# Attention backward on one core: S in three column tiles of 32 query rows, dP in two of 64 and 32

## The chip, the cores and the metric

The kernel runs on one core of a Trainium2 chip. The metric is the device time in microseconds. Two runs of the kernel before took 1706.85 and 1711.59 us, median 1709.22.

## The reference

Two attention blocks, A and B, of the same shape are computed forward, their outputs are concatenated, and all gradients are returned for a given output gradient. For each block:

```python
B, Sq, D = 8, 96, 640
H, Sk, Dh = 32, 512, 128
q = (x @ wq).reshape(B, Sq, H, Dh).transpose(0, 2, 1, 3)
scores = einsum("bhqd,bhkd->bhqk", q, k_cache) * Dh ** -0.5
p = softmax(scores)
o = einsum("bhqk,bhkd->bhqd", p, v_cache)
out = o.transpose(0, 2, 1, 3).reshape(B, Sq, H * Dh) @ wo
...
# vjp: gradients of x, k_cache, v_cache, wq and wo of both blocks
```

All tensors are bfloat16. There are 2 x 32 x 8 = 512 pairs of head and batch element, each with 96 query rows and 512 keys.

## The kernel before

The kernel walks over ticks, one for each pair (head h, batch element b), block A first and then block B. The function `build_block` registers the pieces of work with an `Emitter` under a tick and a slot; the emitter sorts them and issues them in that order. The pieces of one pair are spread over several ticks by the offsets in `OFF`, so that in one tick PE works on S of one pair, on P of an earlier one and on dS of a still earlier one. Work of a head as a whole (projections, transposes, weight gradients) lies in between.

For one pair the stages are as follows.

- K and V are loaded for two batch elements at a time (`c_ld`, L266, on SP's queue). Their transposes come from a DMA transpose (`c_xt`, L275) into KT and VT, or, for about half of the pairs, K is transposed by PE (`c_s1`, L285) and copied by DVE to `KT_pe` (L287).
- S (`c_s2a`, L298) is one product: the stationary side is the 128 x 96 slice of `QT_h`, the moving side is KT with 512 columns. The result `S_ps` is 96 x 512 in float32, one PSUM bank. DVE takes the negated row maximum `negm` (L300).
- ACT computes the exponential with row sums, `E_sb` (L310); DVE inverts the sums, `rinv` (L320); POOL multiplies, `P_sb` (L329).
- PE transposes P (L365), ACT copies it to `PT_sb` (L378); O comes from V and PT (L359) and goes to `OD` by ACT (L375). dV comes from P and dO (L389), and ACT copies it (L392).
- POOL forms `prod` = O times dO (L407). dP (`c_s6`, L417) is one product: the stationary side is the 128 x 96 slice of `dOT_h`, the moving side VT with 512 columns. Directly behind it on PE comes `dl_ps` (L419), with one moving column, which sums `prod`. DVE makes `dS_sb` = (dP - dl) * P (L421).
- PE transposes dS (L346), DVE copies it (L348), dQ comes from K and the transposed dS (L340). dK comes from dS and Q (L432), and ACT copies it (L435).
- The results dV and dK go out by DMAs issued on POOL's queue (L398).

Around these stand the products of a head: Q and dO projections (`q_ps`, L243), transposes (`n_ps` L258, `nat_ps` L455, `woT_ps` L210, `wqT_ps` L216), weight gradients (`dwo_ps` L470, `dwq_ps` L490), and the output and dx sums over a group of heads (`o_ps`, L512).

All PSUM tiles come from one pool of eight banks (`bank`). S and what follows from it down to P are given a higher priority (`tc.high_priority`), which the framework uses when it orders each engine's instructions. Each `nc.tensor.matmul` becomes a weight load of the stationary side and a product. PE runs them in program order; a load may run while the product before it is still running.

Of the kernel before, what the change touches and what calls it, by code (L numbers as in the profile page):

```python
# [53 lines left out]
def build_block(tc, em, tick0, blk, x, kc, vc, wq, wo, g_all, out_all, dx, dk, dv, dwq, dwo, ident, ones, pools, HG=6, first=True, groups=None):  # L54
    nc = tc.nc
    B, Sq, D = x.shape
# [19 lines left out]
    while t0 < T:  # L76
        w = 512 if T - t0 >= 512 else (256 if T - t0 >= 256 else (128 if T - t0 >= 128 else T - t0))
# [4 lines left out]
    while c0 < D:  # L82
        w = 512 if D - c0 >= 512 else (256 if D - c0 >= 256 else 128)
# [14 lines left out]
    def bank(shape, dt, name):  # L98
        return ps.tile(shape, dt, name=name, tag="bank")
# [191 lines left out]
    def c_s2a(h, b):  # L291
        def f():
            with tc.high_priority(PRIO_OFF):
                st = CS[(blk, h, b)]
                hs = HS[(blk, h)]
                tok = slice(b * Sq, (b + 1) * Sq)
                S_ps = bank([Sq, Sk], F32, "S_ps")
                nc.tensor.matmul(S_ps[:], hs["QT_h"][:, tok], st["KT"], start=True, stop=True)  # L298
                negm = wk.tile([Sq, 1], F32, name="negm", bufs=3)
                nc.vector.tensor_reduce(negm[:], S_ps[:], axis=AX.X, op=ALU.max, negate=True)  # L300
                st["S_ps"], st["negm"] = S_ps, negm
        return f
# [108 lines left out]
    def c_s6(h, b):  # L411
        def f():
            st = CS[(blk, h, b)]
            hs = HS[(blk, h)]
            tok = slice(b * Sq, (b + 1) * Sq)
            dP_ps = bank([Sq, Sk], F32, "dP_ps")
            nc.tensor.matmul(dP_ps[:], hs["dOT_h"][:, tok], st["VT"], start=True, stop=True)  # L417
            dl_ps = bank([Sq, 1], F32, "dl_ps")
            nc.tensor.matmul(dl_ps[:], st["prod"][:], ones[:, 0:1], start=True, stop=True)  # L419
            dS_sb = wk.tile([Sq, Sk], BF16, name="dS_sb", bufs=3)  # L420
            nc.vector.scalar_tensor_tensor(dS_sb[:], dP_ps[:], dl_ps[:, 0:1], st["P_sb"][:], op0=ALU.subtract, op1=ALU.mult)  # L421
            st["dS_sb"] = dS_sb
        return f
# [318 lines left out]
```

## Time and profile before

| what | value |
|---|---|
| runs | 1706.85 and 1711.59 us, median 1709.22 |
| profiled execution | span 1699.8 us from the first to the last instruction |
| PE products | 22024, busy 1675.7 us (99%) |
| PE weight loads | 22024, busy 1343.8 us (79%) |
| ACT, DVE, POOL busy | 1405.2, 1329.8, 1040.3 us |
| S products (L298) | 512, two groups of 268 and 244 by the source of KT, mean 380 and 379 ns |
| dP products (L417) | 512, mean 382 ns |
| weight loads for S and dP | 512 each, mean 122 and 123 ns |
| DMA | 423.05 MB, mean 249 GB/s |
| granted TensorE clock | 0.998 of full |

The profile shows one execution. It has no time of that execution other than its span, which lies 9.4 us below the median of the runs; that much lies around the instructions. A duration of a product is from its start to its modelled end, and products overlap; the distance from one start to the next tells how long PE is taken by it. PE and PEld are two rows of one engine: the products and the loads of their stationary sides.

### The profile page before, as it was taken

Reading aid. Unit: us, or ns where it says so; the run is one execution under the profiler, and the core shown is the slowest. Engines: PE = TensorE matmul, PEld = TensorE weight load, DVE = VectorE, ACT = ScalarE, POOL = GpSimd, SP = SyncE. Lnnn points to the kernel's source line nnn. Section 1 sums busy time; section 2 is a strip of 40 time slices with the busy share of each in tenths; the row PEclk is TensorE's granted clock in tenths of the full one; section 3 lists DMA queues with packets and bytes.
Section 4 is the critical chain, followed back from the end, with each engine's and each line's share of the span. In section 5 each row is a group of like instructions: output and inputs, shape, how many; then the busy total and the mean of one; then the engine's idle time right before and its main releaser. Section 6 shows DMA issues by size and latency. Waiting matters only on the chain.

```text
span 1699.8 us, 56567 instructions
## 1 busy us (share of the span) xinstructions
PE 1675.7 (99%) x22024; PEld 1343.8 (79%) x22024; DVE 1329.8 (78%) x3052; ACT 1405.2 (83%) x3518; POOL 1040.3 (61%) x1747
## 2 busy tenths in 40 slices
PE   8999999999999999999999999999999999999999
PEld 7877778778778778777778877887788778778876
DVE  6887678878788878787778876787788778878877
ACT  6998889869869869878768998897799679878975
POOL 3676567646647647656566764675576557656754
PEclk9999999999999999999999999999999999999999
DMA  9999999999999999999999999999899989999994
GB/s 256 252 259 250 258 225 260 262 242 243 262 221 252 268 238 259 225 251 237 281 256 269 273 270 248 238 289 248 218 261 276 237 221 261 281 217 240 263 247 141
DMA packets 600429, 423.05 MB, mean 249 GB/s; under 512 B 419360, under 2 KB 557984, under 8 KB 600160
## 3 DMA queue, kind: packets, MB, share of 16 engines
q1 hardware_dynamic: 546576, 242.08, 72.2%
q0 software_dynamic: 53584, 177.35, 32.7%
q8 instruction: 173, 2.83, 0.7%
q14 instruction: 96, 0.79, 0.2%
HBM read 161.09 MB, written 159.12 MB: 188 GB/s over the span
## 4 chain that ended last, share of the span: by engine, by line
PE 89%; DMA 4%; ACT 3%; issue 1%; DVE 1%; POOL 0%; SPq 0%; DVEq 0%; ACTq 0%; POOLq 0%
PE q_ps L243 12%; PE o_ps L512 12%; PE dwo_ps L470 6%; PE dV_ps L389 6%; PE dK_ps L432 6%; PE S_ps L298 6%; PE dP_ps L417 6%; PE dwq_ps L490 6%; PE x_ps L340 5%; PE x_ps L365 5%; PE dst_ps L346 5%; PE x_ps L359 5%; PE kT_ps L285 3%; PE n_ps L258 3%; PE nat_ps L455 2%; DMA VT<-V_sb 1%
## 5 line engine op out<-in xcount | busy, mean ns | idle before, releaser
L329 POOL TENSOR_SCALAR P_sb<-E_sb,rinv 96x512 bf16<-96x512 bf16 x512 | 352.6, 689 | 567.8 <-DVE rinv L320 559.2
L310 ACT ACTIVATE E_sb<-S_ps,negm 96x512 bf16<-96x512 f32 x512 | 351.0, 686 | 187.6 <-DVE negm L300 181.9
L421 DVE SCALAR_TENSOR_TENSOR dS_sb<-dP_ps,dl_ps,P_sb 96x512 bf16<-96x512 f32 x512 | 382.1, 746 | 60.9 <-PE dl_ps L419 54.6
L300 DVE TENSOR_REDUCE negm<-S_ps 96x1 f32<-96x512 f32 x512 | 347.6, 679 | 50.9 <-PE S_ps L298 46.6
L435 ACT ACTIVATE dK_sb<-dK_ps 128x512 bf16<-128x512 f32 x512 | 302.1, 590 | 63.4 <-PE dK_ps L432 56.5
L392 ACT ACTIVATE dV_sb<-dV_ps 128x512 bf16<-128x512 f32 x512 | 311.6, 609 | 0.0
L378 ACT ACTIVATE PT_sb<-x_ps 128x384 bf16<-128x384 bf16 x512 | 253.1, 494 | 0.0
L512 PEld LDWEIGHTS <-OD 128*128 128x128 bf16 x1536 | 132.2, 98 | 100.4 <-issue 1.0
L398 POOL DMA_DIRECT2D out_dram<-dV_sb x256 | 194.9, 761 | 11.8 <-issue 8.6
L398 POOL DMA_DIRECT2D out_dram<-dK_sb x256 | 195.0, 762 | 9.1 <-issue 4.4
L389 PE MATMUL dV_ps<-dOnat_h,P_sb 96*128 96x128 bf16 x2048 | 198.2, 219 | 0.8 <-DVE dOnat_h L160 0.6
L417 PE MATMUL dP_ps<-VT,dOT_h 128*96 128x512 bf16 x512 | 195.4, 382 | 3.0 <-DMA VT<-V_sb 3.0
L432 PE MATMUL dK_ps<-Qnat_h,dS_sb 96*128 96x128 bf16 x2048 | 198.1, 219 | 0.1
L407 POOL TENSOR_TENSOR prod<-OD,dOT_h 128x96 bf16<-128x96 bf16 x512 | 184.2, 360 | 13.8 <-ACT OD L375 12.6
L348 DVE COPY dST_sb<-dst_ps 128x384 bf16<-128x384 bf16 x512 | 177.1, 346 | 10.5 <-PE dst_ps L346 10.3
L365 PE MATMUL x_ps<-ident,P_sb 96*128 96x96 bf16 x2048 | 172.0, 205 | 0.8 <-POOL P_sb L329 0.3
L359 PE MATMUL x_ps<-PT_sb,V_sb 128*128 128x96 bf16 x2048 | 172.3, 206 | 0.2 <-ACT PT_sb L378 0.2
L346 PE MATMUL dst_ps<-ident,dS_sb 96*128 96x96 bf16 x2048 | 172.3, 206 | 0.2 <-DVE dS_sb L421 0.2
L340 PE MATMUL x_ps<-dST_sb,K_sb 128*128 128x96 bf16 x2048 | 171.0, 206 | 1.3 <-ACT dK_sb L435 0.8
L375 ACT ACTIVATE OD<-x_ps 128x192 bf16<-128x192 f32 (+1 forms) x515 | 167.9, 326 | 3.9 <-PE x_ps L340 3.9
L320 DVE RECIPROCAL rinv<-rowsum 96x1 f32<-96x1 f32 x512 | 79.9, 156 | 106.0 <-ACT E_sb L310 100.4
L340 PEld LDWEIGHTS <-K_sb 128*128 128x128 bf16 x2048 | 131.1, 98 | 25.1 <-issue 1.6
(84 smaller groups left out, 3744.4 us busy)
## 6 DMA issues: line engine op xcount, KB each, us to landing
out_dram<-dV_sb POOLq DMA_DIRECT2D x256, 256.0 KB, 5.2
out_dram<-dK_sb POOLq DMA_DIRECT2D x256, 256.0 KB, 5.3
K_sb<-in_A_k_cache_dram SPq DMA_DIRECT2D x128, 256.0 KB, 5.3
V_sb<-in_A_v_cache_dram SPq DMA_DIRECT2D x128, 256.0 KB, 5.2
K_sb<-in_B_k_cache_dram SPq DMA_DIRECT2D x128, 256.0 KB, 5.0
V_sb<-in_B_v_cache_dram SPq DMA_DIRECT2D x128, 256.0 KB, 4.9
out_dram<-dwo_sb POOLq DMA_DIRECT2D x63, 160.0 KB, 4.8
out_dram<-dwq_sb POOLq DMA_DIRECT2D x31, 320.0 KB, 6.1
```

The lines of the kernel that those rows point to most:

```text
L300: nc.vector.tensor_reduce(negm[:], S_ps[:], axis=AX.X, op=ALU.max, negate=True)
L310: nc.scalar.activation(E_sb[:], st["S_ps"][:], ACT.Exp, bias=st["negm"][:], scale=1.0, accum_out=rowsum[:])
L329: pinned(nc.gpsimd.tensor_scalar(P_sb[:], st["E_sb"][:], st["rinv"][:], 0.0, op0=ALU.mult, op1=ALU.add))
L340: nc.tensor.matmul(dQT_ps, st["K_sb"][:, c, :], st["dST_sb"][:, c * Sq:(c + 1) * Sq], start=(c == 0), stop=(c == KC - 1))
L389: nc.tensor.matmul(dV_ps[:, c * 128:(c + 1) * 128], P_sb[:, c * 128:(c + 1) * 128], hs["dOnat_h"][:, b * 128:(b + 1) * 128], start=True, s ...
L392: nc.scalar.activation(SB[(blk, h, b // 2, "v")][:, b % 2], dV_ps[:], ACT.Identity, scale=1.0)
L398: pinned(nc.gpsimd.dma_start(dst[b - 1:b + 1, h].rearrange("b (p c) d -> p b (c d)", c=KC), SB.pop((blk, h, b // 2, which))[:]))
L417: nc.tensor.matmul(dP_ps[:], hs["dOT_h"][:, tok], st["VT"], start=True, stop=True)
L421: nc.vector.scalar_tensor_tensor(dS_sb[:], dP_ps[:], dl_ps[:, 0:1], st["P_sb"][:], op0=ALU.subtract, op1=ALU.mult)
L432: nc.tensor.matmul(dK_ps[:, c * 128:(c + 1) * 128], dS_sb[:, c * 128:(c + 1) * 128], hs["Qnat_h"][:, b * 128:(b + 1) * 128], start=True, s ...
L435: nc.scalar.activation(SB[(blk, h, b // 2, "k")][:, b % 2], dK_ps[:], ACT.Identity, scale=1.0)
L512: nc.tensor.matmul(o_ps[:], src[:, t * 128:(t + 1) * 128], rhs, start=(hh == 0), stop=(hh == groups[g] - 1))
```

## The change

S is computed by three products, each for 32 of the 96 query rows, and dP by two, for 64 and 32 rows. Every product takes its own slice of the stationary side and writes its own rows of the same PSUM tile. The moving side is the same in all of them. A product whose output has 32 or 64 rows uses as many columns of the array, at the position given by the first output row: S uses 128 x 32 parts at columns 0, 32 and 64, dP a 128 x 64 part at column 0 and a 128 x 32 part at column 64. Nothing else is edited.

```diff
@@ c_s2a
                 S_ps = bank([Sq, Sk], F32, "S_ps")
-                nc.tensor.matmul(S_ps[:], hs["QT_h"][:, tok], st["KT"], start=True, stop=True)
+                for j in range(0, Sq, 32):
+                    nc.tensor.matmul(S_ps[j:j + 32, :], hs["QT_h"][:, b * Sq + j:b * Sq + j + 32], st["KT"], start=True, stop=True)
                 negm = wk.tile([Sq, 1], F32, name="negm", bufs=3)
@@ c_s6
             dP_ps = bank([Sq, Sk], F32, "dP_ps")
-            nc.tensor.matmul(dP_ps[:], hs["dOT_h"][:, tok], st["VT"], start=True, stop=True)
+            for j, w in ((0, 64), (64, Sq - 64)):
+                nc.tensor.matmul(dP_ps[j:j + w, :], hs["dOT_h"][:, b * Sq + j:b * Sq + j + w], st["VT"], start=True, stop=True)
             dl_ps = bank([Sq, 1], F32, "dl_ps")
```

## The prediction

> **What bounds the kernel now.** I read the head of the page first: which engine is full, and at which clock.
>
> ```profile
> span 1699.8 us, 56567 instructions
> PE 1675.7 (99%) x22024; PEld 1343.8 (79%) x22024; DVE 1329.8 (78%) x3052; ACT 1405.2 (83%) x3518; POOL 1040.3 (61%) x1747
> PEclk9999999999999999999999999999999999999999
> PE 89%; DMA 4%; ACT 3%; issue 1%; DVE 1%; POOL 0%; SPq 0%; DVEq 0%; ACTq 0%; POOLq 0%
> ```
>
> PE is busy for 99% of the span at full clock in every slice, and it holds 89% of the chain that ended last. A busy PE can still be waiting inside its pipeline, so the next view is the list of who waited for whom on PE; its longest entries are these.
>
> ```profile
> PE dP_ps L417 <- DMA VT<-V_sb: 3.0, 2, 2.4
> PE tp_ps L134 <- DMA ld_tmp<-in_grad_out_dram: 2.7, 1, 2.7
> PE S_ps L298 <- DMA KT<-K_sb: 2.1, 1, 2.1
> ```
>
> All waits of PE together are under 20 us. So time is set by how fast products follow each other, which is read from start times in the timeline, not from durations. This is PE in an ordinary tick:
>
> ```profile
> 805.51 0.34 PE L365 MATMUL x_ps<-ident,P_sb 96*128 96x96 bf16 x4
> 805.68 0.39 PE L389 MATMUL dV_ps<-dOnat_h,P_sb 96*128 96x128 bf16 x4
> 805.90 0.38 PE L417 MATMUL dP_ps<-VT,dOT_h 128*96 128x512 bf16 x1
> 806.12 0.16 PE L419 MATMUL dl_ps<-ones,prod 128*96 128x1 bf16 x1
> 806.15 0.49 PE L455 MATMUL nat_ps<-ident,OD 128*128 128x128 bf16 x6
> ```
>
> Four products of 128 columns take 0.22 us from start to start, 55 ns each; dP with 512 columns takes 0.22 us; dl with one column 0.03 us, though it lasts 0.16. The distance follows the number of moving columns: (220 - 55) / (512 - 128) = 0.43 ns a column, with a floor of about 26 ns. It does not ask how many columns the stationary side has: S and dP have 96 of them, the others 128. The rest of a duration (380 - 216 = 164 ns for dP, the same as the whole of dl) overlaps the next product. I use 216 ns for the stream of one 512-column product.
>
> How weights are loaded is seen where a product leaves no time for it:
>
> ```profile
> 39.84 0.38 PE L417 MATMUL dP_ps<-VT,dOT_h 128*96 128x512 bf16 x1
> 39.84 0.13 PEld L419 LDWEIGHTS <-prod 128*96 128x96 bf16 x1
> 40.06 0.17 PE L419 MATMUL dl_ps<-ones,prod 128*96 128x1 bf16 x1
> 40.06 0.12 PEld L298 LDWEIGHTS <-QT_h 128*96 128x96 bf16 x1
> 40.09 0.40 PE L298 MATMUL S_ps<-KT_pe,QT_h 128*96 128x512 bf16 x1
> ```
>
> The load for the next product begins when the present one starts, and 30 ns (26 unrounded) after its load S starts. So loads of 0.12 us are pipelined too, and hidden except for the floor.
>
> **What the change adds.** In the program as built, PE's order is that of before with each S replaced by three load-and-product pairs and each dP by two: 3 x 512 = 1536 products and 1536 loads more. S uses a part of the array 32 columns wide at columns 0, 32 and 64; dP uses one 64 wide at 0, then one 32 wide at 64. All else uses the full 128. Every piece still moves all 512 columns of K or V, so the work saved is nil: a tile of 32 query rows streams as long as one of 96. The queues of SP and POOL are unchanged; on DVE some hundred neighbouring instructions change places. I cost those at nothing, because DVE is idle for 22% of the span; with that cover gone each would cost at most one DVE instruction, 0.7 us, some 70 us in all.
>
> **Term 1, further starts of S.** Low bound: a tile starts as soon as its weights are in, 26 ns after the last one (the dl row), and streams beside it: 2 x 26 = 52 ns. High bound: it waits for the stream before, as every product in the trace does: 2 x 216 = 432 ns. I take the low end: the three write different rows of one bank and hold different columns of one mode, so nothing that the rows show in use is shared but the moving operand. That choice is worth (432 - 52) x 512 = 195 us. The Trainium skill, "TensorE: Matmul & The Clock Gate", section "Measured speedup vs the span model", says that tiles in different columns run together, three of them 2.38 times as fast as in sequence, about 4 ns apart. By it this term would be 8 ns; no row here can show it.
>
> **Term 2, the second start of dP.** The bounds are 26 and 216 ns. Here the two pieces have different widths, so they lie in two modes of the array, and I take 216: they follow each other.
>
> **Term 3, changing the width.** S goes from 128 to 32 and back, two changes; dP goes to 64, to 32, to 128, three. The trace shows no such change: all its products use the whole array. Low bound 0: the new product starts on the heels of the old. High bound 190 ns: everything of the old product ends first (164 ns after its stream), and then the new weights are loaded (26). Between these I take 80 ns, by the rows of the durations. A one-column product lasts 164 ns and a load of 96 columns 123, of which 96 x 0.43 = 41 are columns and 82 the way in; 164 - 82 is about 80 ns, what a product has to do in the array and behind it once its last column is there. If the way in may overlap and the array must be empty, that is the gap. The Trainium skill speaks against this change here: "TensorEngine Tiling (Array Packing)", section "Key Properties", says that changing the tiling mode drains the engine, tile changes within a mode do not. It has no duration; by it the zero end of this term would be out.
>
> **The sum.** S: 52 + 2 x 80 = 212 ns. dP: 216 + 3 x 80 = 456 ns. Together 668 ns, 512 times: 342 us. All of it lies on the path, since PE has no idle time to take it. Span 1699.8 + 342 = 2042 us. The median of the runs, 1709.2, lies 9.4 us above the profiled span; with that, 2051 us, which I give as 2050.
>
> **Who waits for later results.** In the tick shown, S starts at 804.33, negm ends at 805.50, E at 806.27, P at 807.36, and PE first uses P at 808.71: 1.3 us of room against 0.2 us of delay, and the following tick is itself later by 0.67. dS ends at 807.21 and is first used at 808.14. Neither becomes a wait; without that room the delay would count once more, 0.2 + 0.46 us a tick at most. ACT's 1405 us are 69% of the new span, so no other engine takes over. The distances between PE starts sum to some 61 us more than the columns account for; with slower PE part of this may vanish, which I leave out.
>
> **Rivals.** *Not slower: tiles side by side, widths changed free.* The mechanism is the early loading seen in the rows: if loads for other columns and modes run under the product before, further starts cost between 0 and 26 ns, three of them 0 to 78 ns a pair of S and dP, 1709 to 1749 us, 1729 in the middle. It decides while the pair costs under 67 ns (34 us / 512), 22 ns a start. For it: no row shows weights being waited for, and 96 and 128 stationary columns alternate without a gap. Against it: five changes of width must cost nothing, and the full-width products use the columns that the tiles use. *In sequence, widths free.* S +432, dP +216, 648 ns x 512 = 332 us: 2041 us. For it: every product in the trace starts after the stream before it. Against it: they all use the same columns. It gives nearly my time, with starts 0.22 us apart inside S. *Full drain.* 190 ns a change: S 52 + 380, dP 216 + 570, 1218 ns x 512 = 624 us: 2333 us. For it: the 164 ns after each stream are real latency; against it: at other boundaries the engine overlaps all of it. *Only dP in sequence, no drain.* 268 ns x 512 = 137 us: 1846 us. Sequence and an 80 ns drain together give 1048 ns, 537 us, 2246 us. That the change doesn't split the products can be left out: the program as built has the pieces.
>
> **How the numbers follow.** Forecast, side by side in S with a partial drain (1900 to 2150): 0.38. In sequence without drain: 0.15. Full drain: 0.17. Sequence and drain: 0.08, most of it below 2335. Only dP in sequence: 0.08. Free: 0.14, of which 0.10 stays below 1743 and 0.04 between there and 1749. The range from 1745 to 2335 leaves out some 0.1 at the bottom and 0.08 at the top, where the full drain comes out heavier than 190 ns. A difference of 2% (34 us) is about what a measurement of this kernel tells from no change. Faster by more has no mechanism: no column streamed is saved and PE is full; 0.02. Within 2%: 0.10. Slower: 0.88.
>
> **What would show it.** In the profile after, PE should have 23560 products and stay near full. In the timeline the three S starts should lie about 0.03 us apart, and the next full-width product should start some 0.3 us after the last of them; dP's second piece should start about 0.30 us after the first. S starts 0.22 us apart mean the sequence; starts 0.4 us apart around each change of width mean the full drain. Pieces of dP close together, or a full-width product 0.22 us after the last tile, make the forecast wrong, and so does a clock below full in the PEclk row, since then gaps would have changed the grant.

## The result and the profile after

The changed kernel takes 2062.97 us (median of two runs, 2061.99 and 2063.95) against 1709.22, a ratio of 1.2083 with a 95% interval of 1.2014 to 1.2151. The forecast was 2050. In the changed file S is line 299, dP 419, dl 421.

The head of the page after, to be read against that of before:

```profile
span 2060.2 us, 59424 instructions
PE 2033.2 (99%) x23390; PEld 1365.1 (66%) x23560; DVE 1358.6 (66%) x3052; ACT 1432.0 (70%) x3518; POOL 1042.2 (51%) x1747
PEclk9999999999999999999999999999999999999999
PE 98%; issue 1%; DVE 0%; DMA 0%; POOL 0%; ACT 0%; SPq 0%; DVEq 0%; POOLq 0%
```

The span is 360 us longer, and PE is still full, at full clock. The other engines have the same number of instructions and nearly the same busy time, now a smaller share. There are 23560 weight loads, 1536 more, as the program has them; 170 product records are missing from the trace. So PE itself takes longer for its work, and the place is seen in the timeline. First PE's products, then its loads, in one stretch of the kernel after:

```profile
1001.29 0.39 PE L390 MATMUL dV_ps<-dOnat_h,P_sb 96*128 96x128 bf16 x4
1001.61 0.72 PE L419 MATMUL dP_ps<-VT,dOT_h 128*64 128x512 bf16 x2
1002.26 0.20 PE L421 MATMUL dl_ps<-ones,prod 128*96 128x1 bf16 x1
1002.33 0.44 PE L134 MATMUL tp_ps<-ident,ld_tmp 128*128 128x128 bf16 x5
1002.61 0.38 PE L243 MATMUL q_ps<-gT,woT_h 128*128 128x512 bf16 x1
1002.92 0.40 PE L299 MATMUL S_ps<-KT,QT_h 128*32 128x512 bf16 x3
```

```profile
1001.61 0.11 PEld L419 LDWEIGHTS <-dOT_h 128*64 128x64 bf16 x1
1001.94 0.09 PEld L419 LDWEIGHTS <-dOT_h 128*32 128x32 bf16 x1 [0.23 <-issue]
1002.26 0.12 PEld L421 LDWEIGHTS <-prod 128*96 128x96 bf16 x1 [0.23 <-issue]
1002.91 0.10 PEld L299 LDWEIGHTS <-QT_h 128*32 128x32 bf16 x3 [0.26 <-issue]
1003.24 0.33 PEld L243 LDWEIGHTS <-woT_h 128*128 128x128 bf16 x3 [0.23 <-issue]
```

From dV to dl PE takes 0.97 us (1001.29 to 1002.26); before it took 0.44 (805.68 to 806.12). The second piece of dP starts 0.33 us after the first, and dl 0.32 after the second. The three pieces of S together last 0.40 us, hardly longer than one product, and the next full-width load begins 0.32 us after their first start. In the rows of the loads the reason stands at the end: at a change of width a load no longer begins with the product before it but, where that has 512 columns, 0.30 to 0.33 us behind its start; the row is idle for 0.23 us or more, and the profile finds nothing that it waited for ("issue").

The start times of the trace give the same distances. These are medians over the 512 pairs, in ns from one product's start to the next. In the kernel after, at least 97% of the steps of each row lie within 4 ns of the median; behind S this leaves out 91 steps of some 548 ns, where the next product is one of the missing records.

| step | before | after | more |
|---|---|---|---|
| a 128-column product, then dP | 56 | 149 | 93 |
| dP's first piece to its second | none | 333 | 333 |
| dP's last product to dl | 220 | 320 | 100 |
| dl to the next product | 26 | 66 | 40 |
| into S, from 128 columns / from 512 | 56 / 215 | 149 / 306 | 93 / 91 |
| between S's pieces, twice | none | 3 | 7 |
| S's last product to the next | 216 | 322 | 106 |
| the full-width product behind S to the one after it | 56 to 215, by its columns | 10 or 11 more; 37 more with 96 stationary columns | 14 on average |

S costs 220 ns more, dP and dl 566, together 786 ns; times 512 that is 402 us. The span grew by 360. The other 42 us come back from small waits that PE had before: dl to its follower, for example, had a mean of 46 ns with a median of 26, which is 10 us of 512 steps; after, nearly all are 66. The section on the prices put together follows these waits up.

### The profile page after: what moved, and what is told of

It is laid out like the page before. It is cut to its first block, busy times and chain, and to the rows that moved or that the text cites. A ratio compares the mean times of both kernels' runs of the same rounds, so it can differ in the third digit from the quotient of the medians.

```text
span 2060.2 us, 59424 instructions
## 1 busy us (share of the span) xinstructions
PE 2033.2 (99%) x23390; PEld 1365.1 (66%) x23560; DVE 1358.6 (66%) x3052; ACT 1432.0 (70%) x3518; POOL 1042.2 (51%) x1747
## 4 chain that ended last, share of the span: by engine, by line
PE 98%; issue 1%; DVE 0%; DMA 0%; POOL 0%; ACT 0%; SPq 0%; DVEq 0%; POOLq 0%
PE dP_ps L419 16%; PE q_ps L243 10%; PE o_ps L514 10%; PE S_ps L299 8%; PE dV_ps L390 6%; PE dwo_ps L472 6%; PE dK_ps L434 5%; PE dwq_ps L492 5%; PE x_ps L366 4%; PE x_ps L360 4%; PE dst_ps L347 4%; PE x_ps L341 4%; PE dl_ps L421 3%; PE n_ps L258 3%; PE kT_ps L285 3%; PE nat_ps L457 2%
## 5 line engine op out<-in xcount | busy, mean ns | idle before, releaser
L419 PE MATMUL dP_ps<-VT,dOT_h 128*64 128x512 bf16 (+1 forms) x1024 | 370.1, 396 | 0.0
L419 PEld LDWEIGHTS <-dOT_h 128*64 128x64 bf16 (+1 forms) x1024 | 101.6, 99 | 169.5 <-issue 116.4
L514 PEld LDWEIGHTS <-OD 128*128 128x128 bf16 x1536 | 117.7, 98 | 112.4 <-issue 40.0
```

The lines of the kernel that those rows point to most:

```text
L419: nc.tensor.matmul(dP_ps[j:j + w, :], hs["dOT_h"][:, b * Sq + j:b * Sq + j + w], st["VT"], start=True, stop=True)
L514: nc.tensor.matmul(o_ps[:], src[:, t * 128:(t + 1) * 128], rhs, start=(hh == 0), stop=(hh == groups[g] - 1))
```

## Experiments

Two theories can give a time near 2063. The width theory: each change of the array's width costs about 0.1 us, pieces of one width run side by side, pieces of different widths follow each other. The count theory: each further product has a price, 354 us / 1536 = 230 ns. Each run below was compared with the kernel before on the same chip.

### S alone in pieces

```diff
 # c_s2a as changed, c_s6 as before
-            for j, w in ((0, 64), (64, Sq - 64)):
...
+            nc.tensor.matmul(dP_ps[:], hs["dOT_h"][:, tok], st["VT"], start=True, stop=True)
```

> Only S is in three pieces of 32 rows; dP is one product. Width theory (a change of the array's width costs some 91 ns plus the load of the first new weights, pieces of one width start 3 ns apart): into S +93 ns, two further starts +7, out of S +104, 204 ns x 512 = 104 us over before, less the small waits of PE that vanish: 1795 to 1815 us, 1808 most likely. Count theory (each further product costs the same, 354 us / 1536 = 230 ns): 1024 further products, +236 us, 1945 us.

Measured: 1785.84 us, 1.0462 (1.0392 to 1.0532). The distances in its trace are those of the table (149 into S behind 128 columns, 3 between pieces, 322 out). The count theory was 160 us too high. The width theory was 9 us too high at its low end: its sum left out the 14 ns behind S, and more of the small waits went than I had taken off (31 us, by the table of prices below).

### dP alone in pieces

```diff
 # c_s6 as changed, c_s2a as before
-                for j in range(0, Sq, 32):
...
+                nc.tensor.matmul(S_ps[:], hs["QT_h"][:, tok], st["KT"], start=True, stop=True)
```

> Only dP is in pieces of 64 and 32 rows; S is one product. Width theory: into dP +93, second piece +333, out to dl +100, the load for dl shown at its follower +40: 566 ns x 512 = 290 us, less vanished waits: 1970 to 2000 us. With the first run the gains must sum to more than the 354 us of both, since the waits can vanish only once. Count theory: 512 further products, +118 us, 1827 us.

Measured: 1953.49 us, 1.1441 (1.1380 to 1.1503), 17 us below the expected range: 38 us of waits went, more than I had taken off. With half as many further products as S it costs three times as much, which no price per product can give. My sentence on the sum was the wrong way round: each single change removes the same waits once, so the two gains, 76 and 244 us, sum to less than 354, not more.

### dP in three pieces of one width

```diff
-            for j, w in ((0, 64), (64, Sq - 64)):
+            for j, w in ((0, 32), (32, 32), (64, 32)):
```

> As the changed kernel, but dP is in three pieces of 32 rows, one width. Width theory: the step of 333 ns between dP's pieces becomes two of 3 ns, so 327 ns x 512 = 167 us less than the changed kernel: 1896 us (1880 to 1910), although there are 512 products more. Count theory: 512 x 230 ns more: 2181 us. If it is VT or dP's place that makes its pieces follow each other, three in sequence: about 2063 + 512 x 0.22 = 2175 us.

Measured: 1894.96 us, 1.1099 (1.1040 to 1.1159): 168 us less than the changed kernel with 512 products more. This settles it against the count theory. PE's timeline of this kernel:

```profile
1000.91 0.40 PE L419 MATMUL dP_ps<-VT,dOT_h 128*32 128x512 bf16 x3
1001.24 0.20 PE L421 MATMUL dl_ps<-ones,prod 128*96 128x1 bf16 x1
```

From dP's first start to dl it is 0.33 us, where the changed kernel needs 0.65. Three pieces now stream in the time of one.

### S in two pieces of two widths

```diff
-                for j in range(0, Sq, 32):
-                    nc.tensor.matmul(S_ps[j:j + 32, :], ...)
+                for j, w in ((0, 64), (64, Sq - 64)):
+                    nc.tensor.matmul(S_ps[j:j + w, :], ...)
```

> As the changed kernel, but S is in pieces of 64 and 32 rows as dP is. Width theory: a third change of width and a stream in sequence are added to S, 333 - 7 = 326 ns x 512 = 167 us more: 2230 us (2210 to 2245). Count theory: 512 products fewer, 118 us less: 1945 us.

Measured: 2230.06 us, 1.3059 (1.2989 to 1.3129), 167 us above the changed kernel with 512 products fewer. The step between S's pieces is 333 ns, as in dP. It is the pair of widths that costs, not the place or the operand.

### Two pieces of 64

```diff
-            dP_ps = bank([Sq, Sk], F32, "dP_ps")
-            for j, w in ((0, 64), (64, Sq - 64)):
-                nc.tensor.matmul(dP_ps[j:j + w, :], ...)
+            dP_ps = bank([128, Sk], F32, "dP_ps")
+            for j in ((0, 64) if b < B - 1 else (0,)):
+                nc.tensor.matmul(dP_ps[j:j + 64, :], hs["dOT_h"][:, b * Sq + j:b * Sq + j + 64], st["VT"], start=True, stop=True)
+            if b == B - 1:
+                nc.tensor.matmul(dP_ps[64:Sq, :], hs["dOT_h"][:, b * Sq + 64:(b + 1) * Sq], st["VT"], start=True, stop=True)
```

> As the changed kernel, but dP's second piece is 64 rows wide too, 32 of them unused, for seven of the eight batch elements; the last keeps 64 and 32. Width theory: pieces of one width run side by side at 64 as at 32, the step of 333 ns becomes 3, out of it some 13 ns more: 317 ns x 448 = 142 us less than the changed kernel, 1921 us (1905 to 1935). Rival: only pieces of 32 run side by side, 64 ones follow each other: 0.22 to 0.33 us apart, 2045 to 2070 us.

Measured: 1920.57 us, 1.1267 (1.1203 to 1.1331). Two pieces of 64 start 3 ns apart, so width 64 runs side by side as 32 does. dl starts 333 ns after them, 13 more than after 32-wide pieces. Its timeline:

```profile
1001.15 0.41 PE L419 MATMUL dP_ps<-VT,dOT_h 128*64 128x512 bf16 x2
1001.49 0.20 PE L423 MATMUL dl_ps<-ones,prod 128*96 128x1 bf16 x1
```

### A change of width with almost no stream, and its control

```diff
 # c_s2a of the kernel before; w = 32 in the first run, 96 in the control
                 S_ps = bank([Sq, Sk], F32, "S_ps")
+                nc.tensor.matmul(S_ps[0:w, 0:1], hs["QT_h"][:, b * Sq:b * Sq + w], ones[:, 0:1], start=True, stop=True)
                 nc.tensor.matmul(S_ps[:], hs["QT_h"][:, tok], st["KT"], start=True, stop=True)
```

> The kernel before, with a product of 32 stationary columns and one moving column put in front of each S, into the first column of S's bank, which S then overwrites. It measures two changes of width with next to no stream. Width theory: into the small product +93, out to S some 107, and the load for S (96 columns, 40 ns) shown: 240 ns x 512 = 123 us less vanished waits: 1810 to 1832 us. Count theory, 230 ns a product: 1827 us as well, but then the next run must be as long.

> The control of the narrow small product: the same one, but with all 96 stationary columns, so of full width. Width theory: 26 ns for the start and at most 16 for the load of S, 42 ns x 512 = 21 us: 1722 to 1732 us. Count theory: 1827 us as with the narrow one.

Measured: the narrow product 1790.86 us, 1.0499 (1.0437 to 1.0560); the full-width one 1710.67 us, 1.0047 (1.0009 to 1.0085). So one product of one column, 512 times, costs 86 us over the median of before in that call (1705.03) when it is 32 wide and 6 us when it is full. Both came out below the expected range, by 19 and 11 us, again by waits that go (36 and 14 us, by the table below). The timelines, narrow first:

```profile
1002.60 0.38 PE L243 MATMUL q_ps<-gT,woT_h 128*128 128x512 bf16 x1
1002.91 0.18 PE L298 MATMUL S_ps<-ones,QT_h 128*32 128x1 bf16 x1
1003.02 0.42 PE L299 MATMUL S_ps<-KT_pe,QT_h 128*96 128x512 bf16 x1
```

```profile
1003.02 0.30 PE L471 MATMUL dwo_ps<-g_nat,Onat 128*128 128x320 bf16 x1
1003.16 0.17 PE L298 MATMUL S_ps<-ones,QT_h 128*96 128x1 bf16 x1
1003.19 0.40 PE L299 MATMUL S_ps<-KT,QT_h 128*96 128x512 bf16 x1
```

The narrow product starts 0.31 us after a 512-column one (216 ns would be the stream), and S 0.11 us after that (median 107). S's own step to its follower grows as well, from 216 to 253 ns. The wide one starts when its predecessor's 135 ns of 320 columns are over, S follows 0.03 us later (median 28 ns), and S's own step grows from 216 to 232. So two changes of width cost 237 ns with next to no stream (1 ns or less): 93 in, 107 out, and 37 behind S. A product more without a change costs 44. The paragraph on Term 3 below parts these into the change and the loads.

### dl in the same width as dP

```diff
 # with dP in three pieces of 32
-            nc.tensor.matmul(dl_ps[:], st["prod"][:], ones[:, 0:1], start=True, stop=True)
+            for j in range(0, Sq, 32):
+                nc.tensor.matmul(dl_ps[j:j + 32, :], st["prod"][:, j:j + 32], ones[:, 0:1], start=True, stop=True)
```

> As dP in three pieces of 32, and dl, which follows it, is in three pieces of 32 rows too, so that the change back to full width comes behind dl and not ahead of it. The number of changes is the same. Width theory: dP to dl shrinks from 320 to 216 ns, dl to the next product is then 6 + 107 + 13 instead of 66: 44 ns x 512 = 22 us less than dP in three pieces. Count theory: 1024 further products, 236 us more.

Measured: 1872.99 us, 1.0986 (1.0924 to 1.1049), 22 us less than with dl at full width, as expected, with 1024 products more. dP to dl is back at 220 ns and the change lies behind dl (99 ns). What goes is the load of 96 columns for dl in the open, for one of 128 columns behind dl that costs 11 ns; the number of changes is the same. By the steps the gain is larger than expected, 49 ns or 25 us; the 22 us come out since fewer small waits went here (39 against 43 us in the table below).

### S and dP in one narrow stay

S of another pair is put directly behind dP, ahead of dl, so that two changes a pair would be left of four; the control moves S in the same way with S and dP as one product each.

```diff
 # with dP in three pieces of 32; c_s2a without high priority
-SLOTS = dict(LOAD=0, S2A=5, S2B=5.5, ...)
+SLOTS = dict(LOAD=0, S2A=50.1, S2B=50.3, ...)
...
+    def c_s6b(h, b):      # dl and dS, split from c_s6
...
+                em.add(ct + OFF["s6"], SLOTS["S6"] + 0.2, c_s6b(h, b))
```

> S and dP both in three pieces of 32 rows, and S of a later pair is moved directly behind dP on PE, ahead of dl, so that both share one stay in the narrow width: two changes of width a pair instead of four. Width theory: against the next run, its control, into 93, further starts 13, out 104, load for dl 40: 250 ns x 512 = 128 us. Against dP in three pieces with S apart it saves some 200 ns, 100 us: 1790 to 1810 us if the move of S costs nothing by itself. Count theory: 2048 further products, 471 us over the control.

> The control: S moved behind dP in the same way, but S and dP one product of 96 rows each. Width theory: as before, 1709 us, plus what the move costs by itself, since S's results come later in the tick: 0 to 50 us.

Measured: 2204.02 us, 1.2881 (1.2800 to 1.2962), and the control 2103.06 us, 1.2280 (1.2188 to 1.2372). Both expectations failed: the move alone costs nearly 400 us. The lists of PE's waits say why, first of the merged kernel, then of the control:

```profile
PE x_ps L365 <- POOL P_sb L329: 273.2, 320, 1.7
```

```profile
PE x_ps L365 <- POOL P_sb L329: 280.9, 343, 2.0
```

S comes so late in its tick that P isn't ready when PE wants to transpose it in the next. The granted clock was lower as well, 0.974 in the merged kernel and 0.986 in the control, where the other kernels have 0.99 to 1.00. The distance between the two, 101 us, is near the 128 expected, but both idle for a third thing and their clocks differ, so it proves little. In the trace the merging itself is seen: behind dP's pieces S starts after 0.23 us, one stream and no change.

```profile
1003.14 0.40 PE L418 MATMUL dP_ps<-VT,dOT_h 128*32 128x512 bf16 x3
1003.37 0.39 PE L298 MATMUL S_ps<-KT,QT_h 128*32 128x512 bf16 x3
```

To take the wait away, all users of P were put one tick later in both:

```diff
-OFF = dict(..., s2=3, s3=3, s4=4, s5=5, s6=6, s7=7, s8=8)
+OFF = dict(..., s2=3, s3=3, s4=5, s5=6, s6=7, s7=8, s8=9)
...
-                P_sb = wk.tile([Sq, Sk], BF16, name="P_sb", bufs=5)
+                P_sb = wk.tile([Sq, Sk], BF16, name="P_sb", bufs=6)
```

> As the kernel with S and dP in one narrow stay, but every stage that uses P comes one tick later (and P has six buffers), so that PE no longer waits for P from POOL. Width theory: against the next run, its control, into 93, further starts 14, out 94, load for dl 39: 240 ns x 512 = 123 us, of which waits may give back up to some 40; and some 100 us less than dP and S in three pieces apart, about 1800 us. If each piece or each narrow product had a price of its own, not each change, the distance to the control would be that of the run with S and dP in three pieces apart to the kernel before, some 185 us.

> The control: S moved behind dP and the users of P one tick later in the same way, S and dP one product of 96 rows each. Width theory: no change of width, so near the kernel before, 1700 to 1740 us.

Measured: 1944.48 us, 1.1403 (1.1327 to 1.1479), and the control 1901.65 us, 1.1154 (1.1092 to 1.1216). The wait for P is gone, but another has come, in the merged kernel and in the control:

```profile
PE dl_ps L427 <- POOL prod L407: 122.5, 169, 2.3
```

```profile
PE dl_ps L427 <- POOL prod L407: 137.4, 191, 2.4
```

Both expectations failed again: about 1800 us for the merged kernel, 1700 to 1740 for the control. The distance is 43 us, of 123 expected; part of the changes' time is now spent where PE would have waited for `prod`: between S and dl, what the steps take beyond those without a wait (309 ns merged, 215 in the control) sums to 146 us in the merged kernel and 204 in the control. As a test of time the four runs are inconclusive. They show in the trace that a second group of the same width needs no change, and, by the controls, how much the order of PE's work was worth: moving S alone cost some 390 us with the users of P in their old tick and some 190 with them one tick later.

### The prices put together

With the medians of each trace, 512 times the sum of the steps' increase over before, against the growth of the profiled span (us):

| kernel | steps | span | less |
|---|---|---|---|
| S alone | 220 ns, 113 | 82 | 31 |
| dP alone | 566 ns, 290 | 252 | 38 |
| both, as changed | 786 ns, 402 | 360 | 42 |
| dP 3 x 32 | 460 ns, 236 | 193 | 43 |
| S 64 + 32 | 1112 ns, 569 | 529 | 40 |
| dP 64 + 64 | 509 ns, 260 | 219 | 41 |
| narrow small product | 237 ns, 121 | 85 | 36 |
| wide small product | 44 ns, 23 | 9 | 14 |
| dl 3 x 32 too | 411 ns, 210 | 171 | 39 |

Where the span grows by 82 to 529 us the prices per step miss it by nearly the same 31 to 43 us. The traces show where this comes back. In the kernel before, what single steps take beyond the median of steps of their kind (the same shapes, with a first product behind a change or behind a one-column product as a kind of its own) sums to 53 us. In the four traces of the experiments that have every product record and S in its place it is 39 us (wide small product), 16 (narrow), 15 (dl 3 x 32) and 13 (dP 64 + 64): 14, 36, 38 and 40 us less, against 14, 36, 39 and 41 in the last column of the table. Much of it lies in the steps from dl to its follower, from dV to dP and from `kT_ps` to `x_ps`. Such time can be given back only once in each kernel. Which event each of those small waits was for was not traced. The spans are compared with one execution of the kernel before; its runs beside the experiments vary from 1695 to 1728 us, so the whole last column could shift by some us.

## Why the prediction was right

**What bounds the kernel.** It held: PE is full, 360 of the 402 us that were added show in the span, and no engine took over. DVE's changed order cost nothing that shows.

**Term 1, further starts of S.** The choice of the low end was right in kind and too high in size: 7 ns for both, not 52. The 26 ns floor that I had read between full-width products doesn't hold between pieces of one width, whose loads and products start 3 ns after each other. The 4 ns of the Trainium skill, "TensorE: Matmul & The Clock Gate", section "Measured speedup vs the span model", are close to it.

**Term 2, dP's second start.** Right: pieces of two widths follow each other, by the stream and a change. The runs with dP at 3 x 32 and at 64 + 64 show that one width in place of two removes the whole 333 ns step.

**Term 3, the change of width.** The kind was right and the size low. A change costs 91 to 93 ns, not 80, beyond the stream of the product before it. No run shows that this gap is what I made the 80 ns from (164 less the 82 of a load's way in), so that they are near each other may be luck. What I left out is that the first load of the new width is then in the open: 13 ns for 32 columns, 27 for 64, 37 to 40 for 96, but only 11 for 128, whose loads are shorter in the rows too (mean 98 ns in the kernel before, against 122 to 125 for 96). The durations show it: 389 ns for a 32-wide piece of 512 columns and 403 for a 64-wide one, where a full-width one lasts 376 behind dl with no load in the open. For dl, the row of the kernel before, then the rows by line and form of the kernel after:

```profile
L419 PE MATMUL dl_ps<-ones,prod 128*96 128x1 bf16 x512 | 84.1, 164 | 0.0
```

```profile
L419 PE MATMUL dP_ps<-VT,dOT_h 128*64 128x512 bf16 x512 | 206.3, 403 | 0.0
L419 PE MATMUL dP_ps<-VT,dOT_h 128*32 128x512 bf16 x512 | 199.4, 389 | 0.0
L421 PE MATMUL dl_ps<-ones,prod 128*96 128x1 bf16 x512 | 104.4, 204 | 0.0
```

dl lasts 204 where it lasted 164, though its work is unchanged. The steps follow from these: 27 + 215 + 91 = 333 from the 64-wide piece to its successor, 13 + 215 + 91 = 319 from the 32-wide one, and 40 + 26 = 66 from dl; and 13 + 93, with the one column of stream, is the 107 from the narrow small product to S. The Trainium skill, "TensorEngine Tiling (Array Packing)", section "Key Properties", says that a change of mode drains the engine and a change of tile doesn't. The runs agree in kind: 91 to 93 ns for the one, 3 ns between pieces for the other. What happens inside the 93 ns they don't show; it is less than the 164 ns for which the old product's record goes on behind its stream.

**The sum.** 668 ns predicted a pair, 786 measured: 60 us too few over 512. In S two errors nearly cancel (212 predicted, 220 measured: 45 too many for the further starts, 53 too few for the two changes and their loads); dP was low by 110. The waits of before, which I had put at some 61 us and left out, gave 42 back. So 342 and 360 lie closer than the terms do; 18 us is a difference of two errors, and that is luck. The 9.4 us that I put around the instructions were misread: each run whose span is on record takes some 1.8 us more than its span. So most of the 9.4, as far as this tells, is that the profiled execution of before was faster than the median. With 1.8 in its place the forecast would have been 2044, not 2050.

**The rivals.** "In sequence, widths free" would have been 2041 us, nearly as good by the time alone; it is wrong, since S's pieces start together and the small narrow product costs 80 us more than the full one. "Free" fails by the same run. "Full drain", 190 ns a change, is twice what was measured. "Only dP in sequence" lacks the drain, and "sequence and drain" fails since S's pieces start together. My signs for the profile were S starts 0.03 us apart (they are 0.003), the next full-width product 0.3 after the last (0.32) and dP's pieces 0.30 apart (0.33).

## What to carry to other kernels

Splitting the stationary side into column tiles doesn't shorten a product, because each tile streams all moving columns; here it only added time. Whether it pays where different work streams side by side no run tried; it would first have to earn back two changes of width. Count the changes of width, not the tiles, and keep all pieces of one group, and small products next to them, in one width. When the total agrees with a forecast, look at the start times before believing the mechanism: here another mechanism, in sequence with widths free, would have given 2041 us, within 22 of the measured total.

## What the runs showed of the hardware

A change of width cost 91 to 93 ns beyond the stream of the product before it in each direction that occurred (128 to 32, 128 to 64, 64 to 32, 32 to 128), where that product had 128 to 512 moving columns. Behind one column it was 94 ns (the 107 less 13 for the narrow product's own load) and 99 behind dl in three pieces.

Behind a change the first weights are loaded in the open, at about 0.42 ns a column for 32, 64 and 96 columns (13, 27, 37 to 40 ns), but in 11 ns for all 128. In one width a load hides behind the product before it where that is long enough: behind the one-column wide small product 16 ns of S's load still showed.

Pieces of one width start 3 ns apart, loads included, well under the 26 ns between full-width products, even when they have one moving column (dl in three pieces).
